# Normalising the first tile between the two statistics halves of the second, with one load moved, in the head of a fused attention and gated-MLP kernel

## The chip, the cores and the metric

The kernel runs on one core of a Trainium2 chip. The metric is the device time of one execution in microseconds (us), as the median of several executions. A profile of one execution gives a span that is 1.7 to 1.8 us shorter than the time of that execution.

The engines are called PE (matrix products), DVE (vector), ACT (activation functions), POOL, and SP (here only an issuer of DMAs).

## The reference

The input x (2048 tokens of 512 numbers, bf16) is normalised per token, and two branches are computed from the result and added to x.

```python
def reference(A_x, A_wqkv, A_wo, B_x, B_w_in, B_w_sp, B_b_sp, B_w_out):
    x = A_x
    xn = _layernorm(x, axis=-1)            # mean 0, variance 1 per token
    return x + _A_ref(xn, A_wqkv, A_wo) + _B_ref(xn, B_w_in, B_w_sp, B_b_sp, B_w_out)
# _A_ref: 32 heads of 16, each token looks at 8 earlier ones (itself included) at distance 2; softmax; output product
# _B_ref: z = gelu(xn @ w_in); the second half of z normalised and mixed over tokens by w_sp; times the first half; @ w_out
```

Only the very beginning matters here: 16 tiles of 128 tokens are normalised, transposed (features on the partitions) and multiplied by the q, k and z weights. The first block is the tiles 0, 4, 8 and 12. I call them tile one, two, three and four of the head. Each goes through the same steps: DVE gathers its statistics (in one piece or in two halves) and joins them (the "aggregate"), ACT takes the reciprocal root of the variance, DVE normalises, PE transposes into a buffer called PSUM, ACT (for tiles three and four ACT and DVE) copies the result to where PE's q matmuls read it.

## The kernel before

Each engine takes its instructions in the order in which the program writes them. These are the parts that the change touches (cut; `...` marks cuts):

```python
    def load_x0(E, tb, h):                       # half of tile one or two
        E.dma_start(xall[:, 0, tb, 256 * h:256 * h + 256], x2[tb * TBS:tb * TBS + P, 256 * h:256 * h + 256])
    def load_wqk(E, s):                          # four weight rows of 128
        for kc in range(C):
            E.dma_start(wqk[:, s, kc], A_wqkv[kc * P:(kc + 1) * P, s * D:(s + 1) * D])
    ...
    for tb in range(2):
        load_x0(SP, tb, 0)
        load_x0(A, tb, 1)
    load_x(A, 0, 2, 4)                           # tiles three and four
    load_wqk(SP, 0)
    load_x(SP, 1, 0, 2)
    ...
    def ln_stats(i, parts=1): ...                # DVE: bn_stats in `parts` pieces, then bn_aggr
    def ln_bn(i): ...                            # DVE: bn_stats of the whole tile
    def ln_agg(i, parts=1): ...                  # DVE: bn_aggr
    def ln_root(sl):                             # ACT: 1/sqrt(variance + eps)
        A.activation(rstd[:, sl], mv[:, sl, 1], ACT.Abs_reciprocal_sqrt, bias=eps_t[:])
    def ln_apply(i): ...                         # DVE: (x - mean) * rstd in place
    def tr(i): ...                               # PE: four 128x128 transposes into PSUM
    def tr_copy(i, pt, c0=0, c1=C):              # ACT: PSUM -> xnT
        A.copy(xnT[:, c0:c1, i * P:(i + 1) * P], pt[:, c0:c1, :])
    def tr_dma(i): ...                           # SP: transposing DMA, used for later tiles
    def q_tile(tb, kcs): ...                     # PE: four q matmuls per weight row, 128 columns each
    ...
    warm_up(10)                                  # PE: matmuls on zeros
    for n in range(2):
        ln_stats(t0[n], 2)
        ln_root(col(t0[n]))
    for n in range(2):
        ln_apply(t0[n])
    pts = [tr(t0[n]) for n in range(2)]
    tr_copy(t0[0], pts[0], 0, 2)
    tr_copy(t0[0], pts[0], 2, 4)
    tr_copy(t0[1], pts[1], 0, 2)
    warm_up(2, 1)
    pqs = [qk_tile() for _ in range(3)]
    ln_stats(t0[2])
    ln_root(col(t0[2]))
    tr_copy(t0[1], pts[1], 2, 4)
    q_tile(0, (0, 1))
    q_tile(0, (2,))
    q_tile(1, (0, 1))
    q_tile(0, (3,))
    ln_bn(t0[3])
    ln_apply(t0[2])
    ln_agg(t0[3])
    pt2 = tr2(t0[2])                             # transposes of tile three
    ...
# later work, by name; z2.0 is the first z2 matmul group, on a tile that tr_dma transposed
ORDER = """
z2.0 z1.3 p1.1 z2.2 zg2.0 p0.1 zg1.3 q2.2 zg2.2 ...
```

Of the kernel before, what the change touches and what calls it, by code (L numbers as in the profile page):

```python
# [16 lines left out]
D = 512  # L17
# [3 lines left out]
C = D // P  # L21
# [48 lines left out]
def kernel(  # L70
# [13 lines left out]
    V = nc.vector  # L84
    A = nc.scalar
    G = nc.gpsimd
    PE = nc.tensor
    SP = nc.sync
# [13 lines left out]
    xall = r_x[:, 0:4 * TB * D].rearrange("p (j b d) -> p j b d", j=4, b=TB)  # L102
# [47 lines left out]
    stats = sb.tile([P, NT, 12], F32, name="stats")  # L150
# [14 lines left out]
    def load_x0(E, tb, h):  # L165
        E.dma_start(xall[:, 0, tb, 256 * h:256 * h + 256], x2[tb * TBS:tb * TBS + P, 256 * h:256 * h + 256])

    def load_wqk(E, s):
        for kc in range(C):
            E.dma_start(wqk[:, s, kc], A_wqkv[kc * P:(kc + 1) * P, s * D:(s + 1) * D])  # L170

    def load_x(E, j, b0, b1):
        for tb in range(b0, b1):
            E.dma_start(xall[:, j, tb], xblk[j][:, tb])

    for tb in range(2):
        load_x0(SP, tb, 0)
        load_x0(A, tb, 1)
    load_x(A, 0, 2, 4)
    load_wqk(SP, 0)  # L180
    load_x(SP, 1, 0, 2)
    load_wqk(SP, 1)
    load_x(SP, 1, 2, 4)
    load_x(SP, 2, 0, 4)
# [22 lines left out]
    def ln_stats(i, parts=1):  # L207
        j, tb = i % 4, i // 4
        w = D // parts
        for h in range(parts):  # L210
            V.bn_stats(stats[:, i, 6 * h:6 * h + 6], xall[:, j, tb, w * h:w * h + w])
        ln_agg(i, parts)

    def ln_bn(i):
        V.bn_stats(stats[:, i, 0:6], xall[:, i % 4, i // 4, :])

    def ln_agg(i, parts=1):
        V.bn_aggr(mv[:, i, :], stats[:, i, 0:6 * parts])

    def ln_root(sl):  # L220
        A.activation(rstd[:, sl], mv[:, sl, 1], ACT.Abs_reciprocal_sqrt, bias=eps_t[:])

    def ln_apply(i):
        j, tb = i % 4, i // 4
        V.tensor_scalar(xall[:, j, tb, :], xall[:, j, tb, :], mv[:, i, 0:1], rstd[:, i:i + 1],
                        ALU.subtract, ALU.mult)

    def tr(i):
        j, tb = i % 4, i // 4
        pt = ps_aux.tile([P, C, P], BF16, name="pt", tag="aux")  # L230
        for c in range(C):
            PE.transpose(pt[:, c, :], xall[:, j, tb, c * P:(c + 1) * P], ident[:])  # L232
        return pt

    def tr_copy(i, pt, c0=0, c1=C):
        A.copy(xnT[:, c0:c1, i * P:(i + 1) * P], pt[:, c0:c1, :])
# [81 lines left out]
    def q_tile(tb, kcs):  # L318
        for kc in kcs:
            for c in range(C):  # L320
                PE.matmul(pqs[c // 2][:, c % 2, tb * P:(tb + 1) * P], wqk[:, 0, kc, c:D:C],  # L321
                          xnT[:, kc, 4 * tb * P:(4 * tb + 1) * P], start=(kc == 0 and tb % 2 == 0), stop=(kc == C - 1 and tb % 2 == 1))
# [14 lines left out]
    def qk_tile():  # L337
        return ps_mm.tile([P, 2, TBS], F32, name="pq", tag="mm")
# [224 lines left out]
    def blk(j):  # L563
        return [4 * tb + j for tb in range(TB)]

    def col(i):
        return slice(i, i + 1)
# [4 lines left out]
    def warm_up(n, b=4):  # L572
        for _ in range(n):
            PE.matmul(pwm[:, 0, 0:b * P].rearrange("p (a b) -> p a b", a=b), warm[:, 0:P],
                      warm[:, 0:P].unsqueeze(1).broadcast_to([P, b, P]), start=True, stop=True)

    t0, i1 = blk(0), blk(1)
    i2, i3 = blk(2), blk(3)
    warm_up(10)
    for n in range(2):  # L580
        ln_stats(t0[n], 2)
        ln_root(col(t0[n]))
    for n in range(2):
        ln_apply(t0[n])
    pts = [tr(t0[n]) for n in range(2)]
    tr_copy(t0[0], pts[0], 0, 2)
    tr_copy(t0[0], pts[0], 2, 4)
    tr_copy(t0[1], pts[1], 0, 2)
    warm_up(2, 1)
    pqs = [qk_tile() for _ in range(3)]  # L590
    ln_stats(t0[2])
    ln_root(col(t0[2]))
    tr_copy(t0[1], pts[1], 2, 4)
    q_tile(0, (0, 1))
    q_tile(0, (2,))
    q_tile(1, (0, 1))
    q_tile(0, (3,))
    ln_bn(t0[3])
    ln_apply(t0[2])
    ln_agg(t0[3])  # L600
# [24 lines left out]
    ln_apply(i1[1])  # L625
    tr_copy(i1[0], pt)
    ln_bn(i1[3])
    ln_apply(i1[2])
    tr_dma(i1[2])
# [100 lines left out]
```

## Time and profile before

| | before |
|---|---|
| time, median of the first 3 runs | 202.14 us (201.85 to 202.32) |
| time, median of 6 runs beside the changed kernel | 202.24 us (201.85 to 202.46) |
| span of the profiled execution | 200.2 us |
| busy PE, DVE, ACT | 98%, 92%, 52% |
| tile one's transposes start on PE | 5.39 us |
| tile three's transposes start on PE | 7.72 us |

PE is busy nearly all the time, and the chain that ended last runs through PE for 95% of the span. Such a kernel is read from where PE still waits: at its start. The lines are shown in the prediction. In the timeline, the first number is the start in us from the begin of the span, the second the length, and the bracket at the end holds the idle time ahead of it with what ended it. In the list of waits, the three numbers are the total, the count and the longest.

The start of tile three's transposes is my measuring point. PE does the same 24 q matmuls before it in both kernels, and after it both programs are the same.

### The profile page before, as it was taken

What the parts mean: (1) busy time and instruction counts of PE and PEld (TensorE: products, weight loads), DVE (VectorE), ACT (ScalarE), POOL (GpSimd) and SP (SyncE); (2) the same over time, 40 slices, a digit from 0 to 9 for tenths busy, and PEclk for the clock granted to TensorE, in tenths of its full rate; (3) what the DMA queues carried; (4) which work ended last, traced back from release to release, by engine and by line L of the source; (5) the groups of instructions that cost most, each with busy time, mean ns of one, the idle gap of its engine ahead of it and who ended that gap; (6) DMA issues with size and microseconds to landing.
All of it is one profiled execution on the core that took longest, in us unless ns stands there. A gap on an engine that the chain in (4) does not pass through costs nothing.

```text
span 200.2 us, 4094 instructions
## 1 busy us (share of the span) xinstructions
PE 195.9 (98%) x1691; PEld 124.1 (62%) x1691; DVE 184.5 (92%) x249; ACT 104.0 (52%) x176; POOL 18.5 (9%) x14
## 2 busy tenths in 40 slices
PE   7999999999999999999999999999999999999994
PEld 2869756665566666666656666666544646664562
DVE  5799999999989999999979999999999999999605
ACT  3586987899899986453431523708402230331400
POOL 3000000899400000000000000000000000000000
DMA  5877689940000095524467999199920295219863
GB/s 162 258 248 174 100 96 274 211 79 3 0 0 3 3 177 94 167 65 100 73 139 170 244 225 170 46 219 177 221 58 0 86 227 144 72 37 124 214 208 105
DMA packets 66562, 25.91 MB, mean 129 GB/s; under 512 B 56496, under 2 KB 66288, under 8 KB 66288
## 3 DMA queue, kind: packets, MB, share of 16 engines
q1 hardware_dynamic: 65824, 25.19, 57.8%
q10 hardware_dynamic: 720, 0.47, 0.7%
q8 instruction: 13, 0.21, 0.5%
q14 instruction: 5, 0.04, 0.1%
HBM read 10.13 MB, written 2.10 MB: 61 GB/s over the span
## 4 chain that ended last, share of the span: by engine, by line
PE 95%; DVE 2%; DMA 1%; issue 0%; SPq 0%; ACT 0%
PE pg L464 37%; PE pz L257 19%; PE pq L315 12%; PE pv L425 7%; PE po L547 7%; PE po L517 6%; PE pq L321 2%; DMA r_x<-in_A_x_dram 1%; PE pa L547 1%; PE pl L375 1%; DVE r_pr L535 1%; PE po L526 1%; PE pb L517 1%; PE pa L315 0%; PE pt L232 0%
## 5 line engine op out<-in xcount | busy, mean ns | idle before, releaser
L464 PE MATMUL pg<-z,r_qk 128*128 128x344 bf16 x448 | 66.8, 309 | 0.0
L464 PEld LDWEIGHTS <-r_qk 128*128 128x128 bf16 x448 | 43.8, 98 | 22.0 <-issue 0.4
L439 DVE TENSOR_TENSOR r_pr<-r_x,r_w 128x2048 bf16<-128x2048 bf16 x32 | 38.4, 1219 | 1.3 <-PE pl L375 1.0
L257 PE MATMUL pz<-w_z,xnT 128*128 128x344 bf16 x256 | 39.3, 309 | 0.0
L443 DVE TENSOR_TENSOR r_pr<-r_pr 128x2048 bf16<-128x2048 bf16 x28 | 33.9, 1218 | 0.4
L257 PEld LDWEIGHTS <-xnT 128*128 128x128 bf16 x256 | 24.9, 98 | 13.4 <-issue 0.4
L470 ACT ACTIVATE gs<-pg,b_col 128x688 bf16<-128x688 f32 x16 | 13.2, 833 | 35.4 <-PE pg L464 26.4
L355 DVE TENSOR_TENSOR r_pr<-r_qk 128x2048 bf16<-128x2048 bf16 x24 | 27.8, 1216 | 0.5 <-ACT r_qk L331 0.5
L315 PE MATMUL pq<-xnT,r_w 128*128 128x512 bf16 (+1 forms) x136 | 24.9, 335 | 0.0
L315 PEld LDWEIGHTS <-r_w 128*128 128x128 bf16 x144 | 15.9, 114 | 7.7 <-issue 0.6
L672 POOL CAST b_col<-b 128x16 f32<-128x16 bf16 x1 | 16.4, 16439 | 33.0 <-DMA b<-in_B_b_sp_dram 33.0
L530 ACT CAST r_qk<-po 128x512 bf16<-128x512 f32 x10 | 5.5, 588 | 22.7 <-PE po L547 22.7
L331 ACT CAST r_qk<-pq 128x1024 bf16<-128x1024 f32 (+1 forms) x16 | 15.4, 984 | 2.5 <-PE pq L315 2.4
L306 ACT ACTIVATE r_uz<-pz 128x688 bf16<-128x688 f32 x16 | 11.7, 740 | 6.6 <-PE pz L257 6.5
L517 PE MATMUL po<-r_lg,r_pr 32*128 32x512 bf16 x192 | 14.5, 375 | 0.0
L425 PE MATMUL pv<-xnT,r_w 128*32 128x512 bf16 x256 | 14.2, 379 | 0.0
L547 PEld LDWEIGHTS <-r_uz 128*128 128x128 bf16 x85 | 8.1, 98 | 9.4 <-issue 1.1
L364 DVE TENSOR_TENSOR r_pr<-r_pr 128x4096 bf16<-128x4096 bf16 x6 | 13.7, 2283 | 0.0
L547 PE MATMUL po<-r_w,r_uz 128*128 128x512 bf16 x60 | 13.6, 380 | 0.0
L281 ACT ACTIVATE junk<-z 128x688 bf16<-128x688 bf16 x16 | 12.4, 774 | 0.1
L275 ACT ACTIVATE z<-pz 128x688 bf16<-128x688 f32 x16 | 11.8, 740 | 1.2 <-PE pz L257 1.2
L425 PEld LDWEIGHTS <-r_w 128*32 128x32 bf16 x256 | 9.5, 138 | 4.2
(85 smaller groups left out, 194.6 us busy)
## 6 DMA issues: line engine op xcount, KB each, us to landing
r_lg<-in_A_wo_dram SPq DMA_DIRECT2D x8, 256.0 KB, 4.0
r_x<-in_A_x_dram SPq DMA_DIRECT2D x12, 128.0 KB, 3.2
out_dram<-r_qk SPq DMA_DIRECT2D x12, 128.0 KB, 2.2
r_w<-in_A_wqkv_dram SPq DMA_DIRECT2D x8, 128.0 KB, 3.5
r_qk<-in_A_x_dram SPq DMA_DIRECT2D x8, 128.0 KB, 2.2
w_z<-in_B_w_in_dram SPq DMA_DIRECT2D x4, 172.0 KB, 5.2
w_z<-in_B_w_in_dram SPq DMA_DIRECT2D x1, 688.0 KB, 5.4
r_w<-in_B_w_out_dram SPq DMA_DIRECT2D x1, 640.0 KB, 7.1
```

What stands on the lines that cost most here:

```text
L257: PE.matmul(pz[:, hh, 0:FHALF], xnT[:, kc, i * P:(i + 1) * P], wz[:, kc, hh * FHALF:(hh + 1) * FHALF], start=(kc == 0), stop=(kc == C - 1))
L315: PE.matmul(pq[:, cc, p0 * P:(p0 + b1 - b0) * P], wqk[:, sd, kc, c0 + cc:D:C], xv[:, kc, b0:b1, j, :], start=(kc == 0), stop=(kc == C - 1))
L331: cast = A.copy(dst, pq[:, :, p0 * P:(p0 + b1 - b0) * P].rearrange("p c (b t) -> p c b t", b=b1 - b0))
L355: prod = V.tensor_tensor(pr[g % 3][:, c].rearrange("p w b t -> p b w t"), q3.unsqueeze(2).broadcast_to([P, TB, 4, P]), k4, ALU.mult)
L364: V.tensor_tensor(pr[g % 3][:, 0:2], pr[g % 3][:, 0:2], pr[g % 3][:, 2:4], ALU.add)
L425: PE.matmul(pv[32 * tb:32 * tb + 32, dd, :], wv[:, kc, 2 * d2 + dd, :], xnT[:, kc, tb * TBS:(tb + 1) * TBS], start=(kc == 0), stop=(kc == ...
L439: V.tensor_tensor(pw_t[n], vp[:, :, off:off + P], a_sb[:, slot_w(w), ts].unsqueeze(1).broadcast_to([P, DH, P]), ALU.mult)
L443: V.tensor_tensor(pw_t[n] if dst is None else dst, pw_t[n], pw_t[m], ALU.add)
L464: PE.matmul(pg[:, hh, 0:FHALF], wsp[n][:, k, :], z2[:, k, hh * FHALF:(hh + 1) * FHALF], start=(k == 0), stop=(k == NT - 1))
L517: PE.matmul(pc, op[32 * tb:32 * tb + 32, d, o * P:(o + 1) * P], wo_r[32 * tb:32 * tb + 32, d, cs], start=(d == 8), stop=False, tile_positi ...
L547: PE.matmul(pc, uT[:, o % 2, m, tb * P:(tb + 1) * P], wout[:, m, cs], start=False, stop=(m == MCH - 3))
L672: G.tensor_copy(b_col[:], b16[:])
```

## The change

Its intent: tile one's normalise stands on DVE behind tile two's statistics, although its reciprocal root is ready long before. The change puts it between the two statistics halves of tile two, so that PE can begin earlier. Tile three's statistics are cut in halves too, to lie around the normalise of tile two. The x of tile four goes from ACT's queue to SP's, between weight rows 2 and 3.

```diff
-    load_x(A, 0, 2, 4)
-    load_wqk(SP, 0)
+    load_x(A, 0, 2, 3)
+    load_wqk(SP, 0, 0, 3)
+    load_x(SP, 0, 3, 4)
+    load_wqk(SP, 0, 3, 4)
 ... (load_wqk and ln_bn get arguments for a part)
-    warm_up(10)
-    for n in range(2):
-        ln_stats(t0[n], 2)
-        ln_root(col(t0[n]))
-    for n in range(2):
-        ln_apply(t0[n])
-    pts = [tr(t0[n]) for n in range(2)]
-    tr_copy(t0[0], pts[0], 0, 2)
-    tr_copy(t0[0], pts[0], 2, 4)
-    tr_copy(t0[1], pts[1], 0, 2)
-    warm_up(2, 1)
+    warm_up(9)
+    ln_stats(t0[0], 2)
+    ln_root(col(t0[0]))
+    ln_bn(t0[1], 0, 2)
+    ln_apply(t0[0])
+    ln_bn(t0[1], 1, 2)
+    ln_agg(t0[1], 2)
+    pt0 = tr(t0[0])
+    tr_copy(t0[0], pt0, 0, 2)
+    ln_root(col(t0[1]))
+    tr_copy(t0[0], pt0, 2, 4)
+    ln_bn(t0[2], 0, 2)
+    ln_apply(t0[1])
+    ln_bn(t0[2], 1, 2)
+    ln_agg(t0[2], 2)
+    warm_up(1)
     pqs = [qk_tile() for _ in range(3)]
-    ln_stats(t0[2])
+    q_tile(0, (0, 1))
+    pt1 = tr(t0[1])
+    tr_copy(t0[1], pt1, 0, 2)
     ln_root(col(t0[2]))
-    tr_copy(t0[1], pts[1], 2, 4)
-    q_tile(0, (0, 1))
     q_tile(0, (2,))
+    tr_copy(t0[1], pt1, 2, 4)
     q_tile(1, (0, 1))
     q_tile(0, (3,))
```

More of the change, by code (lines that the diff above doesn't have):

```diff
@@ L166, in load_x0, with load_wqk @@
         E.dma_start(xall[:, 0, tb, 256 * h:256 * h + 256], x2[tb * TBS:tb * TBS + P, 256 * h:256 * h + 256])
-    def load_wqk(E, s):
-        for kc in range(C):
+    def load_wqk(E, s, k0=0, k1=C):
+        for kc in range(k0, k1):
             E.dma_start(wqk[:, s, kc], A_wqkv[kc * P:(kc + 1) * P, s * D:(s + 1) * D])
@@ L212, in ln_stats, with ln_bn @@
         ln_agg(i, parts)
-    def ln_bn(i):
-        V.bn_stats(stats[:, i, 0:6], xall[:, i % 4, i // 4, :])
+    def ln_bn(i, h=0, parts=1):
+        w = D // parts
+        V.bn_stats(stats[:, i, 6 * h:6 * h + 6], xall[:, i % 4, i // 4, w * h:w * h + w])
     def ln_agg(i, parts=1):
```

## The prediction

> **What bounds the kernel now.** I read the page's busy times first, then the chain that ended last in order of time, then the timeline of each engine over the first 14 us, which is where every changed line runs. From the page:
>
> ```profile
> PE 195.9 (98%) x1691; PEld 124.1 (62%) x1691; DVE 184.5 (92%) x249; ACT 104.0 (52%) x176; POOL 18.5 (9%) x14
> PE 95%; DVE 2%; DMA 1%; issue 0%; SPq 0%; ACT 0%
> ```
>
> PE is the bound. The waits of PE over the whole span are only two, both at the start:
>
> ```profile
> PE pwm L574 <- DVE warm L189: 1.1, 1, 1.1
> PE pt L232 <- DVE r_x L225: 0.4, 1, 0.4
> ```
>
> The start-to-start distances agree: after 5.39 us matmuls follow each other at 0.056 us per 128 columns, 0.146 per 344, 0.217 per 512, with some ten gaps of about 0.1 us. So whatever moves PE's work around 8 us moves the end by the same amount: the head must be worked out to a tenth of a microsecond, and nothing later can give much back. The chain in the head:
>
> ```profile
> 1.27 2.77 DMA r_x<-in_A_x_dram
> 4.04 0.02 issue
> 4.06 0.77 DVE stats L211 x2
> 4.83 0.02 issue
> 4.85 0.22 DVE mv L218
> 5.07 0.02 issue
> 5.09 0.30 ACT rstd L221
> 5.40 0.03 issue
> 5.42 0.42 DVE r_x L225
> 5.84 0.05 issue
> 5.89 0.40 PE pt L232 x4
> ```
>
> It runs through the second tile: its x lands at 4.04, two half statistics, aggregate, reciprocal root on ACT, normalise at 5.42, transposes at 5.89. PE's part of the timeline:
>
> ```profile
> 5.39 0.90 PE L232 MATMUL pt<-ident,r_x 128*128 128x128 bf16 x8 [0.36 <-DVE r_x L225]
> 6.13 0.28 PE L574 MATMUL pwm<-warm 128*128 128x128 bf16 x2
> 6.25 1.64 PE L321 MATMUL pq<-xnT,r_w 128*128 128x128 bf16 x24
> 7.72 0.39 PE L242 MATMUL pt<-ident,r_x 128*128 128x128 bf16 x4
> ```
>
> The first tile's root is ready at 4.29 (3.998 + 0.295), but its normalise starts only at 4.98, behind the second tile's statistics; that is what the change attacks. My measuring point is the third tile's transposes, at 7.72: before it PE must run the same 24 q matmuls in both kernels. In the 24 there is one wait: the ninth starts 0.160 after the eighth instead of 0.056, when weight row 2 has landed (6.75). So the change can gain at most 0.5 us of start and 0.1 us of weight wait.
>
> **What the Trainium skill says.** "TensorE: Matmul & The Clock Gate", Part 1, gives start-to-start 426.7 ns (512 columns) cold and 55.6 / 215.7 ns (128 / 512) warm, and some 3.4 us of activity before the change. The trace agrees: warm-up matmuls follow at 0.427 from 1.06 to 4.02, then 0.217, and q matmuls at 0.056. So nine warm-ups (the ninth starts at 4.44) should still bring PE to full clock. "DMA: Bandwidth & Descriptors", "Issuing engines are not separate DMA queues", says that DMAs of several engines run on the same 16 DMA engines and only the sequencer's issue time is saved; here an issue takes 0.33 to 0.45 us, and SP's issues are also stopped by landings, as below. "Perfetto Trace Analysis", "Optimizing Scalar/DVE Operations", says that splitting instructions may let work complete sooner where an engine causes bubbles; the split here is for that. "ScalarE: Activation LUTs", "What ACT_TABLE_LOAD costs", has about 1283 ns; the trace has 1.28 (2.70 to 3.99), just ahead of the first root.
>
> **The loads.** In SP's waits stands:
>
> ```profile
> SPq L170 <- DMA r_x<-in_A_x_dram: 0.4, 1, 0.4
> ```
>
> The program has eight landing semaphores in turn: the ninth DMA, weight row 2, is issued at 3.08 once an x half has landed at 3.06; without that wait it would go at about 2.65 (2.20 + 0.45). In the change the fourth tile's x takes the ninth place: row 2 goes at 2.65, ahead of it, x at 3.08 instead of 2.22, row 3 at 3.45 as before. Bytes in front of the fourth x are then those in front of row 2 before, so I estimate it to land at about 6.75 (was 5.57), row 2 at about 6, row 3 unchanged at 7.08. The halves of the second tile (4.04 and 4.23) stand ahead of all this in both queues and don't move. ACT issues one DMA fewer and its table load comes 0.45 us earlier; that helps only the first root, by some 0.05 us, which is not the last condition.
>
> **The instructions.** Start-to-start on DVE from the trace: half statistics to the next operation 0.345; half statistics to their own aggregate 0.446; aggregate to the next 0.10 to 0.126; full statistics to the next 0.578; normalise to the next 0.329, its duration 0.40. Root and copy on ACT: root 0.295 long, next operation 0.204 after its start; half copy 0.372 long, next 0.268 after. Handover DVE to PE 0.058, PE to ACT 0.037, ACT to PE 0.051, ACT or DVE to each other 0.035. Four transposes: the last starts 0.177 after the first and ends 0.219 later.
>
> The change adds two statistics instructions (two halves for one full, twice) and removes one warm-up; the rest is order. Worked forward:
> - DVE: first half of tile two 4.06 (landing, as before); normalise tile one 4.41 to 4.80; second half 4.735; aggregate 5.18 to 5.39.
> - PE: transposes of tile one 4.86 instead of 5.39, a gain of 0.53; last ends 5.26; one warm-up fits into the idle time.
> - ACT: copy of tile one's first half 5.29 to 5.67. The root of tile two, ready at 5.42, stands behind it: 5.56 to 5.86 (was 5.09 to 5.39). Second copy 5.77 to 6.12.
> - PE: eight q matmuls 5.71 to 6.16, against 6.25 before.
> - DVE: first half of tile three 5.29; normalise tile two waits for the root: 5.89 to 6.30, against 5.42 before. Second half 6.22, aggregate 6.66 to 6.87, full statistics of tile four 6.77 if its x is there, normalise of tile three from 7.35.
> - PE: transposes of tile two 6.36, against 5.89: **0.47 later**. Four q matmuls 6.58 to 6.81. Last transpose ends 6.76, copy 6.79 to 7.17. The next eight q matmuls need this copy: 7.22, after 0.4 us of idle PE; then four more, 12 x 0.0558 = 0.67: PE arrives at 7.89.
> - ACT: root of tile three stands behind that copy, 7.06 to 7.36; DVE normalises tile three 7.39 to 7.80; its transposes can start at 7.86.
>
> Both roads meet at about 7.88 to 7.89, against 7.72: **0.16 us later**. From there the order is the same, each operation of DVE and ACT that PE needs (root of tile four, half copies, normalise of tile four) is shifted by nearly the same 0.16, and so is the rest. The early start is real, but tile two pays for it: its normalise waits for a root that queues behind a copy. Sum: -0.53 (earlier start) and -0.10 (weight row) are gains; new idle PE between 4.65 and 7.22 more than uses them up. 202.14 + 0.16 = 202.30.
>
> **The rivals.**
> 1. The early start carries through: if copies and roots fell better, up to 0.5 us would be gained, 201.6 to 201.8. For it: PE's only avoidable wait is that one. Against it: tile two's chain after its landing at 4.23 has become longer, not shorter.
> 2. The fourth x becomes the wait: at 6.75 it lands just where DVE wants it (6.77). If it comes 0.1 to 0.3 us later, tile three's normalise, which is behind it on DVE, and all PE work move as much: 202.4 to 202.6. For it: single DMA engines finish late (row 2's last parts landed at 6.61 and 6.75 though most were in at 6.0). Against it: ACT's queue is emptier.
> 3. The later halves of x land earlier because the fourth x no longer competes: at most 0.2 us of the wait at 4.04 could go, as DVE is occupied until 3.83. That makes 202.1 to 202.2. Against it: they were in the queues earlier.
> 4. The clock gate turns later because PE now idles in between: some transposes or q matmuls at half rate, up to 0.5 us more.
> 5. All is hidden by slack later: 202.14. Against it: PE's waits show no slack.
>
> **Range and chances.** The forward working gives 202.30; I put the middle slightly lower, at 202.25, since a better order than I see would pull down. The three runs before span 0.47 us by themselves. Rival 3 and half of 1 set the low end, 201.8; rival 2 the high end, 202.65. Two per cent is 4 us, while the whole head up to 7.72 us can give or cost less than 1 us: within 2% is nearly sure, 0.98, and 0.01 on each side.
>
> **What would show it.** In the profile after: transposes of tile one near 4.86; the root of tile two started directly behind an ACT copy near 5.56; transposes of tile two near 6.36; idle PE of about 0.4 us before the second tile's q matmuls near 7.22; third tile's transposes near 7.88; weight row 2 no longer waited for; everything after 8 us shifted equally. I am wrong if tile two's transposes start before 6.2, if ACT puts the root before the copy, if the fourth x lands after 6.9, or if PE's later waits absorb the shift.

## The result, and the profile after

The changed kernel took 202.39 us (median of 6 runs, 202.10 to 202.50), beside 202.24 us of the kernel before in the same rounds. The ratio is 1.0006, with a 95% interval from 0.9993 to 1.0019. By the times alone the two kernels are equal; a loss of 0.12 us (0.06%) is the best guess. What the change did must be read from the profiles.

The busy times of the changed kernel, and its waits of PE over the span:

```profile
PE 196.4 (98%) x1689; PEld 124.2 (62%) x1689; DVE 184.5 (92%) x250; ACT 104.0 (52%) x176; POOL 18.1 (9%) x14
...
PE pwm L577 <- DVE warm L191: 1.1, 1, 1.1
PE pq L324 <- ACT xnT L239: 0.2, 1, 0.2
```

The wait for the normalise of tile one (0.4 us before) is gone. In its place stands a wait of q matmuls for an ACT copy. The chain in order of time, from tile one's transposes on:

```profile
5.08 0.47 PE pt L235 x4
5.56 0.43 PE pwm L577
5.98 0.03 issue
6.02 0.61 PE pq L324 x8
6.62 0.04 issue
6.66 0.41 PE pt L235 x4
7.08 0.02 issue
7.10 0.38 ACT xnT L239
7.48 0.04 issue
7.52 0.83 PE pq L324 x12
8.36 0.22 PE pt L245 x4
```

Tile two's transposes (L235 at 6.66) stand at 5.89 in the chain before. The copy of tile two at 7.10 then holds the twelve q matmuls at 7.52. Why tile two is late is in the timelines of ACT and DVE:

```profile
5.59 0.37 ACT L239 COPY xnT<-pt 128x256 bf16<-128x256 bf16 x1 [1.15 <-PE pt L235]
5.86 0.30 ACT L224 ACTIVATE rstd<-mv,eps_t 128x1 f32<-128x1 f32 x1
...
6.19 0.41 DVE L228 TENSOR_SCALAR r_x<-r_x,mv,rstd 128x512 bf16<-128x512 bf16 x1 [0.43 <-ACT rstd L224]
```

The aggregate of tile two ended at 5.47, but its root started at 5.86, right behind tile one's copy, and DVE sat 0.43 us idle until then. Tile one's transposes began at 4.95, 0.45 us earlier than before. Tile three's began at **8.19, 0.47 us later** than before. The first z2 matmul came 0.37 us later (22.04 against 21.67), and the span was 0.4 us longer.

This pair of profiles shows a larger loss than the times do. The experiments were to show which part of it belongs to the change.

### The profile page after: what moved, and what is told of

It is laid out like the page before. It is cut to its first block, busy times and chain, and to the rows that moved or that the text cites. A ratio compares the mean times of both kernels' runs of the same rounds, so it can differ in the third digit from the quotient of the medians.

```text
span 200.6 us, 4091 instructions
## 1 busy us (share of the span) xinstructions
PE 196.4 (98%) x1689; PEld 124.2 (62%) x1689; DVE 184.5 (92%) x250; ACT 104.0 (52%) x176; POOL 18.1 (9%) x14
## 4 chain that ended last, share of the span: by engine, by line
PE 97%; DVE 1%; issue 0%; ACT 0%
PE pg L467 37%; PE pz L260 19%; PE pq L318 12%; PE pv L428 7%; PE po L550 7%; PE po L520 6%; PE pwm L577 2%; PE pq L324 2%; PE pa L550 1%; PE pl L378 1%; DVE r_pr L538 1%; PE po L529 1%; PE pb L520 1%; PE pt L235 1%; PE pa L318 0%
```

## The experiments

The theory: the early start of tile one is paid for by tile two, whose root queues behind a copy and whose transposes come late. The rivals: the moved load of tile four has become a wait; the clock of PE turned later for a reason that is not the order; and a later wait hides part of it.

All experiments gave correct results. The table has the reading of each profile. "Clock" says when back-to-back matmuls of PE turned from 0.427 us (512 columns) or 0.107 us (128 columns) apart to half of that. Twelve of the fourteen traces hold a clock event that gives the time, always in keeping with the distances; for the other two (before, third whole) it is read from the distances alone. "Wait for the transposing DMA" is the time that the first z2 matmul stood behind PE's own readiness (13.85 us after tile three's transposes).

| kernel | order | clock turned, us | tile three's transposes | wait for the transposing DMA | first z2 matmul | ratio of times to before |
|---|---|---|---|---|---|---|
| before | before | 4.4 | 7.72 | 0.10 | 21.67 | 1 |
| before, again | before | 6.12 | 7.89 | 0.40 | 22.14 | 1.0003 (0.9990 to 1.0017) |
| load only | before | 5.83 | 7.73 | 0.26 | 21.85 | 1.0003 (0.9990 to 1.0015) |
| rows in pairs | before | 4.57 | 7.99 | 0.35 | 22.19 | 1.0008 (0.9995 to 1.0020) |
| z swap | before | 6.39 | 7.74 | none | 21.59 | 0.9984 (0.9970 to 0.9997) |
| z swap, again | before | 5.44 | 7.67 | none | 21.53 | 0.9984 (0.9967 to 1.0000) |
| changed | changed | 5.95 | 8.19 | 0 | 22.04 | 1.0006 (0.9993 to 1.0019) |
| changed, again | changed | 6.31 | 8.14 | 0 | 22.00 | 1.0005 (0.9991 to 1.0019) |
| order only | changed | 5.68 | 8.14 | 0 | 22.00 | 1.0000 (0.9988 to 1.0013) |
| z swap, changed | changed | 6.42 | 8.14 | none | 21.99 | 0.9997 (0.9985 to 1.0010) |
| root first | changed, mended | 4.89 | 8.12 | 0.60 | 22.57 | 1.0001 (0.9987 to 1.0014) |
| root and transposes, z swap | changed, mended | 6.80 | 8.08 | none | 21.93 | 0.9988 (0.9972 to 1.0003) |
| third whole | changed | about 5.35 | 8.31 | 0.29 | 22.45 | one run, state unknown |
| no warm-ups | changed | 9.83 | 8.82 | 0 (PE itself ready only after 14.28) | 23.09 | one run, state unknown |

### The load alone, and the order alone

```diff
 # load_only: the kernel before with
-    load_x(A, 0, 2, 4)
-    load_wqk(SP, 0)
+    load_x(A, 0, 2, 3)
+    load_wqk(SP, 0, 0, 3)
+    load_x(SP, 0, 3, 4)
+    load_wqk(SP, 0, 3, 4)
 # order_only: the changed kernel with this taken back
```

> The kernel before with only the load part of the change (fourth x between weight rows 2 and 3 on SP). Theory: weight row 2 lands near 5.7 to 6.0 us and the 0.10 us wait of PE in front of the ninth q matmul goes; the fourth x lands near 6.5 to 6.75 and DVE takes its statistics at 6.57, so the third tile's transposes start at 7.61 (x in time) to 7.8 (x late), against 7.72. Rival 'the fourth x becomes the wait': a gap on DVE in front of the fourth tile's statistics and transposes at 7.75 or later. Time 202.1 to 202.3, no difference that the rounds can show.

> The changed kernel with the loads of the kernel before (fourth x on ACT, weight row 2 held back until an x half has landed). Theory that the order of normalise, root and copy alone costs the time: third tile's transposes where the changed kernel has them, 7.9 (full clock early) to 8.2 (late), since row 2, landing at 6.75, is needed only by matmuls that sit in idle PE time. Rival that the fourth x's later load costs it: transposes 0.1 us or more earlier than in the changed kernel at the same clock. Time 202.3 to 202.5.

With the load alone, weight row 2 landed at 5.67 and the ninth q matmul no longer waited. (With the old loads, row 2 landed between 6.31 and 6.92 us in five profiles, and PE waited for it in two of them, 0.10 and 0.13 us; so the wait that the load was to remove comes and goes by itself.) But tile four's x landed at 6.63, and DVE waited 0.16 us for it, as DVE's timeline of this kernel shows:

```profile
6.31 0.18 DVE L220 BATCH_NORM_AGGREGATE mv<-stats 128x2 f32<-128x6 f32 x1
6.66 0.69 DVE L217 BATCH_NORM_STATS2 stats<-r_x 128x6 f32<-128x512 bf16 x1 [0.16 <-DMA r_x<-in_A_x_dram]
7.27 0.40 DVE L227 TENSOR_SCALAR r_x<-r_x,mv,rstd 128x512 bf16<-128x512 bf16 x1
```

The normalise of tile three stands behind these statistics and ends at 7.66, so that the transposes could start at 7.72. They came at 7.73, and PE's own road ends there too: its 24 q matmuls began at 6.40, late because the clock was late, and ran without a wait. With the old loads, an equally late clock and no wait for row 2 (z swap) they came at 7.74. So the profile doesn't show the new wait to be the one that holds; an earlier clock would meet it at 7.72 (an estimate from this trace). Either way the load alone gained nothing in this order.

With the order alone, tile three's transposes came at 8.14, as in the other profiles of the changed order at a late clock (8.14 to 8.19). So the load did not make the loss in the head; the order did. Weight row 2, landing at 6.35 here, was not needed before 6.85. By the times this kernel lost nothing (1.0000), which the section on the second road bears on.

### The weight rows in two loads

```diff
 # the kernel before with
-    load_wqk(SP, 0)
+    for k0 in (0, 2):
+        SP.dma_start(wqk[:, 0, k0:k0 + 2], A_wqkv[k0 * P:(k0 + 2) * P, 0:D].rearrange("(k p) f -> p k f", p=P))
```

> The kernel before with the four q weight rows loaded by two DMAs of two rows each, so that the first eight DMAs cover all that the head needs and none is held back for a landing. Theory: the second pair is issued near 2.2 instead of 3.08 and 3.45, the wait of 0.10 in front of the ninth q matmul goes and the third tile's transposes start at 7.61 against 7.72. Rival: the 256 KB pair lands as a whole only after 6.25 and PE waits for it, transposes at 7.72 or later. Time 202.0 to 202.2, 0.1 us less than before.

My theory fell here and the rival held. The second pair landed as a whole at 7.02, not row by row, and PE's waits from 6 to 8 us have the line

```profile
PE pq L322 <- DMA r_w<-in_A_wqkv_dram: 0.3, 1, 0.3
```

with the ninth q matmul at 7.07 instead of 6.80 and tile three's transposes at 7.99. Fewer and larger loads issue earlier, but what is needed first then waits for all of it.

### The root ahead of the copy

```diff
 # the changed kernel with
     pt0 = tr(t0[0])
-    tr_copy(t0[0], pt0, 0, 2)
     ln_root(col(t0[1]))
+    tr_copy(t0[0], pt0, 0, 2)
     tr_copy(t0[0], pt0, 2, 4)
```

> The changed kernel with the root of tile two ahead of the copy of tile one on ACT. Theory (tile two's normalise is held by a root that queues behind a copy): root starts 0.035 after its aggregate ends, near 5.42 to 5.5 instead of 5.86; normalise of tile two near 5.8 instead of 6.19; third tile's transposes about 0.15 earlier than with the copy first at the same clock, 7.74 to 7.85. Rival (the clock gate's late turn alone made the changed kernel later): transposes stay at 7.9 to 8.2 unless the gate turns early. Time about 202.2.

The root did start 0.035 us after its aggregate (at 5.556), and tile two's normalise started at 5.885 instead of 6.19. But tile three's transposes came at 8.12, nearly where they were. PE's timeline of this kernel:

```profile
6.16 0.61 PE L324 MATMUL pq<-xnT,r_w 128*128 128x128 bf16 x8 [0.55 <-ACT xnT L239]
6.61 0.39 PE L235 MATMUL pt<-ident,r_x 128*128 128x128 bf16 x4
6.83 0.39 PE L324 MATMUL pq<-xnT,r_w 128*128 128x128 bf16 x4
7.45 0.83 PE L324 MATMUL pq<-xnT,r_w 128*128 128x128 bf16 x12 [0.24 <-ACT xnT L239]
```

The copy of tile one, now behind the root, releases the q matmuls only at 6.16, and tile two's transposes stand behind eight of them in PE's order, so they start at 6.61, although the normalise of tile two had ended near 6.30. Moving the root alone moved the wait to the next queue. The x of this run also landed a little late (first half 3.15, against 3.09 and 3.04 in the two profiles of the changed kernel). My number for this kernel was wrong by some 0.3 us, mainly because I hadn't followed the effect on PE's order. The rival's number was met, but not its reason: here the clock had turned at 4.89, ahead of all transposes, and they ran 0.056 us apart.

```diff
 # root_tr_swap: also
-    q_tile(0, (0, 1))
+    q_tile(0, (0,))
     pt1 = tr(t0[1])
+    q_tile(0, (1,))
     tr_copy(t0[1], pt1, 0, 2)
 # and the swap of the two z2 tiles that is told below
```

> The changed kernel with three orders mended: root of tile two ahead of tile one's copy on ACT, transposes of tile two after four q matmuls on PE instead of eight, and the two z2 tiles swapped. Theory (tile two's path through root, transposes and copy is what keeps PE idle; moving the root alone only pushed the wait to the transposes behind eight q matmuls): root of tile two 0.035 after its aggregate, q matmuls from 6.05, transposes of tile two near 6.3, no idle PE in front of tile two's q matmuls, third tile's transposes at 7.6 to 7.8, held by DVE's normalise of tile three, against 8.14 in the changed kernel with a late clock; time 0.2 to 0.4 us below the changed kernel with the swap alone, about that of the kernel before with the swap. Rival (the late clock's slow transposes make the loss): third tile's transposes at 8.0 or later.

The transposes of tile two now started at 6.35, but tile three's came at 8.08, not at 7.6 to 7.8. By its number the rival was right, and the clock had not turned yet, so the four q matmuls and the four transposes went at half rate (0.107 us apart), the copy of tile two started at 6.99, and PE still waited 0.18 us for it. With transposes at full rate the copy would have started some 0.24 us earlier (0.15 less from first to last, 0.095 less to the end of the last), which gives an estimate of about 7.85 by PE's road. But there is a second cause in this profile, which the theory and its rival left out. Tile four's x, moved to SP's queue, landed at 6.90, and DVE stood idle for it:

```profile
6.93 0.69 DVE L218 BATCH_NORM_STATS2 stats<-r_x 128x6 f32<-128x512 bf16 x1 [0.40 <-DMA r_x<-in_A_x_dram]
```

Tile three's normalise stands behind these statistics. From their start to that of the normalise it is 0.61 us (in the profile of the load alone), the normalise takes 0.41, and the handover to PE 0.06; so by DVE's road I estimate no start before about 8.0, whatever the clock. So three things lie together on this path: the queues around tile two, slow transposes when the clock is late, and the moved load once the order is mended. The mended order with the old loads was not run. This mended version is not better than the kernel before with the same swap (0.9988 against 0.9984), and 0.18 us below the changed kernel with the swap by the ratios, a little less than expected.

### The clock

```diff
 # after_again, before_again: no edit
 # no_warm: the changed kernel with
-    warm_up(9)
+    warm_up(1, 1)
```

> The changed kernel, unchanged, once more, for its profile. Theory that the clock's turn falls by chance: warm-ups turn from 0.427 to 0.216 us apart at another time than in the first profile (where the warm-up at 5.35 was still slow); if early (near 4.4), the transposes of tile one take 0.18 from first to last instead of 0.295 and the third tile's transposes come at 7.85 to 8.0. Rival that one warm-up less makes it late: turn again after 5.35 and the third tile's transposes near 8.2.

> The kernel before, unchanged, once more: an A/A comparison and a second profile. Theory that the clock's turn falls by chance: it may turn anywhere from 4.4 to 6 us; if late, the first tile's transposes take 0.32 from first to last and the q matmuls start near 6.4 instead of 6.25, the third tile's transposes near 7.85. Rival that ten warm-ups always turn it by 4.45: same figures as in the first profile, 7.72. Time equal, ratio within 0.999 to 1.001.

> The changed kernel without its first nine warm-ups (one short one instead), to see what the clock costs in the head by itself. Theory that PE's own activity turns the clock: transposes and q matmuls 0.107 us apart until some 3.4 us of work have passed, so third tile's transposes near 9 us or later, span 0.8 us or more above the changed kernel. Rival (the turn doesn't depend on what PE has done): same figures as with the warm-ups, 8.0 to 8.2.

The kernel before, unchanged, turned its clock at 4.4 us in one profile and at 6.12 us in the next. There the ten warm-ups ended 0.4 us later and the transposes of tiles one and two took 0.32 us from first to last instead of 0.18. They stand in PE's timeline as

```profile
5.29 1.01 PE L232 MATMUL pt<-ident,r_x 128*128 128x128 bf16 x8
```

So a late turn needs no change of the program. In the profiles with warm-ups, the turn lies between 4.4 and 6.8 us, and in most of them after 5.3: at 4.4 to 6.39 in the six with ten warm-ups ahead of the transposes, at 4.89 to 6.80 in the seven with nine. Whether nine make a late turn more frequent, these few profiles can't say. These are PE's lines of the changed kernel's second profile:

```profile
4.89 0.62 PE L235 MATMUL pt<-ident,r_x 128*128 128x128 bf16 x4
5.30 0.63 PE L577 MATMUL pwm<-warm 128*128 128x512 bf16 x1
5.97 0.75 PE L324 MATMUL pq<-xnT,r_w 128*128 128x128 bf16 x8
6.62 0.40 PE L235 MATMUL pt<-ident,r_x 128*128 128x128 bf16 x4
```

Four transposes take 0.62 us at 4.89 and 0.40 us at 6.62: the turn lies within the eight q matmuls between them.

Without the warm-ups, PE ran at half rate until about 9.8 us and tile three's transposes came at 8.82; the single execution (state unknown) took 203.44 us with a span of 201.6, 1.1 us longer than that of the changed kernel's second profile (200.5). (I had expected the transposes near 9 us or later.) Counted from the start of PE's steady work (4.62 us here, 1.06 with warm-ups), the turn came after 5.2 us here and after 3.4 to 5.7 us there; that speaks for PE's own activity turning the clock, on one profile without warm-ups. The last q matmuls ahead of tile three's transposes, at half rate:

```profile
6.92 2.10 PE L324 MATMUL pq<-xnT,r_w 128*128 128x128 bf16 x16
```

Sixteen q matmuls took 2.10 us here, one idle stretch of 0.24 us included.

### The third tile's halves

```diff
 # the changed kernel with
-    ln_bn(t0[2], 0, 2)
     ln_apply(t0[1])
-    ln_bn(t0[2], 1, 2)
-    ln_agg(t0[2], 2)
+    ln_bn(t0[2])
+    ln_agg(t0[2])
```

> The changed kernel with the third tile's statistics in one piece after the second tile's normalise. Theory that the halves are worth something: the first half lies in DVE's wait for the root and costs nothing, the whole one starts after the normalise, aggregate of tile three 0.25 later, normalise of tile three and its transposes 0.2 us later than in the changed kernel, 8.35 at a late clock. Rival (tile three's root is held by ACT's copy anyway): transposes where they were, 8.14 to 8.19.

Tile three's aggregate came at 7.18 (6.93 in the changed kernel's second profile) and its transposes at 8.31 against 8.14, with PE idle before them. So the halves are worth 0.17 us within this order: the first half lies in DVE's wait for the root. This rests on one profile of each, both with slow transposes of tile one; third_whole ran once, so its time says nothing.

### A second road

One reading was not in my prediction: the first z2 matmul. In the second profile of the kernel before, and of the changed kernel, PE around 22 us:

```profile
22.14 0.46 PE L257 MATMUL pz<-w_z,xnT 128*128 128x344 bf16 x2 [0.24 <-DMA xnT<-r_x]
```

```profile
22.00 0.60 PE L260 MATMUL pz<-w_z,xnT 128*128 128x344 bf16 x3
```

The changed kernel was 0.26 us later at tile three's transposes (8.14 against 7.89) and yet 0.14 us earlier here. The matmul reads a tile that SP transposes by DMA. That DMA is issued 10.6 us after tile three's transposes in all profiles with warm-ups, and takes 2.95 to 3.78 us to land; PE is ready after 13.85 us. Whenever the DMA takes more than about 3.2 us, PE waits. What comes after the first z2 matmul is nearly the same in all: from it to the end of the span 178.53 to 178.57 us pass in twelve of the fourteen profiles, and 178.66 in two (rows in pairs, and root and transposes mended), for a reason that I didn't look for. So nearly all of a difference in span is there when the first z2 matmul starts. The swap lets PE take first a tile that was transposed long before:

```diff
-z2.0 z1.3 p1.1 z2.2 zg2.0 p0.1 zg1.3 q2.2
+z1.3 z2.0 p1.1 z2.2 zg1.3 p0.1 zg2.0 q2.2
```

> The kernel before with the first two z2 tiles and their gelus swapped, so that the first z2 matmul reads a tile whose transposing DMA landed near 17 us and not the one that lands near 21.6. Theory that a second road bounds this place (transposing DMA of the third block's first tile): first z2 matmul starts 13.85 us after the third tile's first transpose, with no wait; in the profiles so far it waited 0.1 (before), 0.26 (loads alone), 0.35 (rows in pairs), 0.6 us (root first). Time 0.1 to 0.3 us less than before. Rival (the wait is a wait for PSUM or ACT, or is given back later): first z2 matmul later than 13.9 us after, or time unchanged.

> The changed kernel with the same swap. Theory: first z2 matmul 13.85 us after the third tile's first transpose; without the second road the whole of the head's loss shows, so this kernel is slower than the other swapped one by 0.15 us (clock early) to 0.5 us (clock late); time about that of before. Rival (the second road hides the loss in the changed kernel, and only there): as fast as the other swapped kernel.

> The kernel before with the swapped z2 tiles, unchanged, once more. Theory: ratio below 1 again, 0.9975 to 0.9995, third tile's transposes 7.6 to 7.9 and the first z2 matmul 13.85 us later without a wait. Rival (the first result was chance): ratio at or above 1.

In both swapped kernels the first z2 matmul came 13.85 us after tile three's transposes, with no wait. Tile three's transposes and the first z2 matmul in the kernel before with the swap, and then in the changed one:

```profile
7.74 0.39 PE L242 MATMUL pt<-ident,r_x 128*128 128x128 bf16 x4
21.59 0.89 PE L257 MATMUL pz<-w_z,xnT 128*128 128x344 bf16 x5
```

```profile
8.14 0.33 PE L245 MATMUL pt<-ident,r_x 128*128 128x128 bf16 x3
21.99 0.60 PE L260 MATMUL pz<-w_z,xnT 128*128 128x344 bf16 x3
```

On the kernel before, the swap gave a ratio of 0.9984 twice (intervals 0.9970 to 0.9997 and 0.9967 to 1.0000), 0.3 us; on the changed kernel 0.9997. This is the cleanest comparison of the two orders: with the second road out of the way, and a late clock in both first profiles, the changed order is 0.41 us later at tile three's transposes (8.14 against 7.74) and at the first z2 matmul (21.99 against 21.59), 0.39 us longer in span (200.54 against 200.15), and 0.26 us slower by the ratios (0.9997 less 0.9984, of 202.2 us; 0.37 by the medians, 202.26 and 201.89). The intervals of the two ratios overlap (0.9985 to 1.0010 and 0.9970 to 0.9997), so the times alone would not prove it. In the first of the two, weight row 2 landed at 6.36 and cost nothing; with the wait of 0.10 or 0.13 us that two other profiles of the old order show, the distance would be that much smaller. The kernel before with the swap is the fastest version that was run, 201.89 and 201.88 us.

## Why the prediction was right or wrong

**The time was right.** 202.25 was predicted, with 201.8 to 202.65; 202.39 was measured. That was partly luck: two errors, a loss in the head that was larger and a later wait that gave some of it back, cancelled in part. So the points matter more than the sum.

- *The early start:* tile one's transposes predicted at 4.86, measured 4.89 and 4.95 (4.87 with other landings). Right.
- *The root behind the copy:* right as a mechanism. It starts 0.27 us after the copy in the profiles, as predicted. Its time was 5.86 and 5.81 instead of 5.56, because the copy itself was later.
- *Idle PE ahead of tile two's q matmuls:* predicted 0.4 us; 7.07 to 7.52 less one matmul of 0.056, which is 0.40. Right.
- *"nine warm-ups (the ninth starts at 4.44) should still bring PE to full clock":* wrong, and with it the size of the loss at 8 us: 7.88 predicted, 8.14 and 8.19 measured. This is the term that was mis-sized. In the second profile the start was only 0.03 us later than predicted but the copy after it 0.25 us, and that offset stays up to tile three: transposes of tile one at half rate. It was rival 4 of the prediction, which I had held to be the exception, because I had one profile of the kernel before and took its turn at 4.4 us for a fixed one. The reason that rival 4 gives, idle PE in between, is not shown: the kernel before turned as late without it.
- *Weight row 2 no longer waited for, fourth x just in time:* right. Row 2 landed at 5.72 and the fourth x at 6.49, both somewhat earlier than I estimated, and neither held anything in the changed kernel. But in the eight profiles with the moved load the fourth x landed anywhere from 6.49 to 6.94. Rival 2 is out for the changed kernel, whose DVE wants it only at 7.06 to 7.10; with the load alone DVE waited 0.16 us for it, and in the mended order 0.40.
- *"adds two statistics instructions" and "removes one warm-up":* wrong as counts, without effect on the sums. DVE's instructions went from 249 to 250: one full statistics became two halves, since tile two's were halves already. PE's went from 1691 to 1689: one warm-up of 512 columns moved behind tile one's transposes, and the two short ones fell away.
- *"PE's waits show no slack"* and *"everything after 8 us shifted equally":* wrong. The wait of 0.1 us at 21.46 in the profile before was among the "some ten gaps of about 0.1 us", and I took it for one of the fixed ones. It is a wait for a DMA that can grow to 0.6 us. In the first pair of profiles it gave back 0.10 us of 0.47; in the second, more than the whole head's loss. The prediction named "if PE's later waits absorb the shift" as a sign of being wrong; in part it came true. This fits that the times differ by only 0.12 us where the swapped kernels differ by 0.26 us, though both differences are of the size of the noise.

What stays open: whether the transposing DMA is shorter because of the changed order (3.05 to 3.13 us in four profiles of it, but 3.42 with the swap and 3.46 with the third tile whole, and 2.95 and 3.78 in the two mended orders; 3.28 to 3.61 in the order before) or by chance. Also open is the size of the loss with an early clock: no profile of the changed order had one, so the predicted 0.16 us was not tested.

## What to carry to other kernels

Moving one tile's work forward between pieces of the next tile's work helps only if the next tile's chain keeps its place in every queue that it crosses; here it crossed DVE, ACT and PE, and lost more in ACT's and PE's order than the first tile won. In a kernel that is bound by one engine from start to end, list also that engine's small waits and what releases each: one that ends with a DMA is a second road, and taking a tile that is ready first cost nothing and gave 0.3 us (in both of two tries, though the second interval reaches 1.0000). A single profile does not show what varies from run to run; before building on the time of a clock turn or of a landing, take a second one of the same kernel.

## What the Trainium skill lacked or had wrong

- "TensorE: Matmul & The Clock Gate", Part 1, "What you observe", has the turn of the clock around 4 us into sustained activity, within 500 ns from run to run. Here the same kernel with ten warm-ups from 1.06 us on turned after 3.4 us in one profile and after 5.1 us in another, and kernels with nine warm-ups and some idle PE turned 3.8 to 5.7 us after the first. (Further down, the same Part tells of one kernel with 6, 11 or 14 slow matmuls in different runs, which is nearer to this than the 500 ns; my prediction passed over it.) The page says in Part 4 that the full clock doesn't engage for transposes. Read as a statement on their rate, that doesn't hold here: the transposes against the identity went 0.107 us apart before the turn and 0.056 us after it, like other matmuls of 128 columns. The rates agree with the page. Its warning that the clock events of the trace can be unreliable is met in one way only: two of fourteen traces hold no event. In the other twelve the time of the event fits the distances of the matmuls (at 6.12 us in the second profile of the kernel before). What misleads is the mean granted clock of the views: it was told as 1.00 between 4 and 5 us in that profile, while its warm-ups were 0.427 us apart, because no event lies ahead of the turn.
- "ScalarE: Activation LUTs", "What ACT_TABLE_LOAD costs", adds a drain of about 1380 ns to the load's 1283 ns. The load takes 1.28 us here, but in the kernel before it starts 0.03 us after ACT's last DMA issue, and the first root starts 0.012 us after its end; at the switch to gelu (22.93 us) the load starts 0.02 us after the operation ahead of it and the first gelu 0.01 us after its end. No drain shows.
- No page that I found has how long a transposing DMA of a 128x512 tile takes from issue to landing (the nearest figure, in "VectorE: DVE Perf Modes", is for a 128x128 tile). Here it is 2.95 to 3.78 us, and this spread is what makes the second road come and go.
